# FNet mixing and a hard-swish MLP on one core: the first pair of batches handled one batch at a time

## The chip, the core and the metric

The kernel runs on one core of a Trainium2 chip. The core has TensorE (PE in the profile, its weight loads listed as PEld), VectorE (DVE), ScalarE (ACT), GpSimd (POOL) and SyncE (SP). Each engine works through its own instructions in program order and waits on semaphores for the others. DMAs are issued from the queues of SP, ACT and POOL and carried by 16 DMA engines. The metric is the device time of one execution in microseconds.

## The reference, cut to what matters

```python
# x: (8, 3008, 256) float32; w_in: (256, 2048) and w_out: (2048, 256), both float64
X = np.fft.fft(x, axis=1)
X = np.fft.fft(X, axis=2)
t = X.real.astype(np.float32).reshape(8 * 3008, 256)
h = t @ w_in
g = h * np.clip(h + 3.0, 0.0, 6.0) / 6.0
out = g @ w_out
```

## The kernel before, in words

The sequence of 3008 is split as 47 x 64. **Stage 1** is the Fourier sum over the 47 (its tables are `F`, and `F0` for the first pair), **stage 2** the one over the 64 with the twiddle factors (tables `T`). The transform over the 256 features is folded into `w_in`: the matrix `C` multiplies `w_in` on TensorE (`fold_w_in`, L663), and the result lies in `W1`. `w_in` and `w_out` come as float64. They are taken apart into exponent and mantissa by ScalarE, VectorE and TensorE (`exponent_a`, `exponent_b`, `exponent_c`, `mantissa`, `join`, L600 to L647) in 16 pieces, each brought in by `load_w` on POOL's queue. The real input's symmetry is used twice: a row and its partner are added and subtracted first (`fold`, L180), where the partner rows are gathered by an indirect DMA (`load_partners`, L170).

The eight batches form four pairs. For a pair, the rows of x are loaded in eight chunks of four columns of the 64 (`XC = 4`, `NXC = 8`), folded, put through stage 1, copied from PSUM to `z` by ScalarE, and written to memory as `zd` by SP. A group of four k1 is then read back as `g` (`load_g`, L305), transposed by the write and the read, and goes through stage 2 (`stage2`, L324), half a group for each call, into `q`. One row of q is needed on all partitions; `spread` (L354) writes it to memory and reads it back as a broadcast `qn`. For the first group `spread_by_pe` does that by products.

**The first pair** runs ahead of everything. Its two batches lie one under the other on 94 partitions, `stage1_first` (L253) multiplies by a block table of 94 x 96, and only the rows of group 0 are written at once. The rest stands in the list `later` and is written in the first MLP steps. Loads and gathers are all on POOL's queue, three chunks ahead. `keep_awake` (L687) issues products of zeros on TensorE: nine at the start, one after each of the first seven chunks.

**The MLP** runs over 4 pairs x 12 chunks (`ck`) x 8 steps (`fc`). A chunk is 4 k1-and-batch columns of 64 with their mirrored ones; before, two k1 for both batches. A step s issues, in the order written by hand:

- what `ahead` holds for it,
- `mlp1` of step s + 2: products u and v (L394) into one of three PSUM buffers, then `activate` on VectorE and ScalarE,
- what `behind` holds for it,
- `combine` of step s + 1 on POOL: three additions of 128 x 512 and 128 x 256 (L457),
- for the chunk before: `finish` at fc = 0 (five additions on POOL), `store` at fc = 1 and fc = 2 (two transposes on VectorE, L548, and eight output DMAs on SP, L554, each),
- `mlp2` of step s: seven products that add up over fc (L487).

The first eight steps (`first_steps`, `second_steps`) differ: the weights are finished between the products. `mix_w_out` makes four more blocks from `w_out` on POOL.

`beside` (L796) is the planner for all other work: `put(t, f, ...)` places a call in front of step t of the pair (or behind its mlp1 with `at=behind`). Stage 2 of later groups, their loads, and the next pair's x loads, folds (on POOL) and stage 1 (L223, four products of 47 rows in the four quarters of the array) are placed there. Since each engine keeps program order, an entry's DMAs stand on SP behind the outputs of earlier steps.

Pools matter as follows: `xpool` has four buffers for x, partners and some weight pieces; `ps_d` is one PSUM bank for stage 1, stage 2 and exponents; `ps_h` has three banks, for u and v first of all; `zpool`, `gpool` and `ypool` have two each.

Of the kernel before, what the change touches and what calls it, by code (L numbers as in the profile page):

```python
# [58 lines left out]
def kernel(  # L59
# [21 lines left out]
    PR0, PZ0 = 2 * N1, 2 * PZ  # L81
    XC = 4
    NS = N2 // 2
    NXC = NS // XC
    KC = 4
# [4 lines left out]
    NG = NCK // 2  # L90
    DH = 32
# [23 lines left out]
    F = consts.tile([P, 5 * PB], F32, name="F")  # L115
    F0 = apool.tile([PR0 + 2, 6 * PZ0], F32, tag="a", name="F0")
# [10 lines left out]
    class Pair:  # L127
        def __init__(self, p):
            self.p = p
            self.x, self.xr, self.y, self.z = {}, {}, {}, {}  # L130
            self.zd = self.zq = None
            self.g, self.q, self.qn = {}, {}, {}
# [3 lines left out]
    ORDER = [NXC - 1] + list(range(NXC - 1))  # L136

    def x_tile(pr, c):
        pool, tag = (spool, "t") if pr.p == 0 and ORDER.index(c) % 3 == 2 else (xpool, "x")
        return pool.tile([PX, XC, D], F32, tag=tag, name="xt")  # L140
# [8 lines left out]
    def load_forward(pr, c):  # L149
        xt = x_tile(pr, c)  # L150
        n = XC if c < NXC - 1 else XC - 1
        if pr.p == 0:
            o = xt[0:PR0 + 2]
            nc.gpsimd.dma_start(out=o[:, 0:n, :], in_=x_pn[0:PR0 + 2, c * XC + 1:c * XC + 1 + n, :])
            if n < XC:
                nc.gpsimd.dma_start(out=o[:, n:XC, :], in_=x_pn[0:PR0 + 2, 0:1, :])
        for b in range(2) if pr.p > 0 else ():
# [12 lines left out]
    def load_partners(pr, c):  # L170
        xr = x_tile(pr, c)
        pr.xr[c] = xr
        i = pr.p * NXC + c
        nr = PX if pr.p > 0 else PR0 + 2
        nc.gpsimd.indirect_dma_start(  # L175
            out=xr[0:nr].rearrange("p n d -> p (n d)"), out_offset=None, in_=x_r,
            in_offset=bass.IndirectOffsetOnAxis(ap=IX[0:nr, i:i + 1], axis=0),
        )

    def fold(pr, c, part, eng):  # L180
        nr = PX - 1 if pr.p > 0 else PR0
# [71 lines left out]
    def stage1_first(pr, c):  # L253
        y = pr.y.pop(c)
        n = XC if c < NXC - 1 else XC - 1

        def table0(i):
            return F0[0:PR0, i * PZ0:(i + 1) * PZ0]

        pt = ps_h.tile([P, 2 * TB], F32, tag="uv", name="pt")[0:PZ0]  # L260
        nc.tensor.matmul(pt[:, 0:n], table0(5), y[:, 0:n, P], start=True, stop=True)
        for k in range(2 if n < XC else 0):
            nc.tensor.matmul(pt[:, n:XC], table0(k + 1), y[:, n + k, P:P + 1], start=(k == 0), stop=(k == 1))

        k = ORDER.index(c)
        pool, tag = (zpool, "z") if k < 2 else (cpool, "c") if k < 5 else (qpool, "q") if k < 7 else (apool, "a")
        z = pool.tile([PZ0, XC, D + 1], F32, tag=tag, name="z")
        nc.scalar.copy(z[:, :, D], pt[:, 0:XC])
        for i in range(XC // 2):
            ps = bank([P, 2, D], "ps1")[0:PZ0]  # L270
            if (c, i) == (NXC - 1, XC // 2 - 1):
                nc.tensor.matmul(ps[:, 0], table0(0), y[:, 2 * i], start=True, stop=False, skip_group_check=True)
                for k, (j, cs) in enumerate([(XC - 1, slice(0, P + 1)), (XC, slice(0, P + 1)),
                                             (XC - 1, slice(P + 1, D)), (XC, slice(P + 1, D))]):
                    nc.tensor.matmul(ps[:, 1, cs], table0(k + 1), y[:, j, cs], start=False, stop=(k % 2 == 1),
                                     skip_group_check=True)
            else:
                nc.tensor.matmul(ps, table0(0), y[:, 2 * i:2 * i + 2, :], start=True, stop=True)
            nc.scalar.copy(z[:, 2 * i:2 * i + 2, 0:D], ps)
# [63 lines left out]
    def spread_by_pe(pr, gr, i, ps, copy=nc.scalar.copy):  # L343
# [7 lines left out]
        if i == 1:  # L351
            del pr.g[gr]
# [677 lines left out]
```

## Time and profile before

| what | value |
|---|---|
| three runs | 1940.03, 1940.06, 1939.75 us; median 1940.03 |
| span of the profiled execution | 1938.6 us |
| VectorE, stage 0 to 20 us / 20 to 40 / 40 to 56 / 56 to 80 | busy 13.0 / 15.2 / 13.7 / 22.6 us |
| DMA in the same stretches | 0.84, 230 GB/s / 0.85, 262 / 0.84, 274 / 0.55, 174 |
| POOL, 100 to 300 us | busy 167 of 200 us |
| L457, c<-a, POOL, 128 x 512 / 128 x 256 | 1250 / 716 ns each |
| L223, stage 1 product of a pair, PE | 601 ns each, 192 instructions |
| L187, L188, L193, L194, fold on POOL, 111 x 508 | 1229, 1058, 1263, 1264 ns |
| L187 and the like, fold on VectorE, 94 x 508 | 660 to 680 ns |
| L707, memset of 128 x 512, VectorE | 485 ns |
| L711, zeros into T, ScalarE | 2 x 2750 ns |
| L604, exponent, ScalarE | 764 ns each, two a piece |

"Busy" counts an engine's own instructions. A product of 32-bit numbers appears as two instructions of TensorE. In a timeline line the first number is the start, the second the extent in us, then engine, line, operation, what is written from what, and the count; in brackets stand idle time before it and what ended it.

### The profile page before, as it was taken

The page shows a single profiled execution, that of the slowest core. Times are in us where ns is not written, and L with a number is a line of the kernel's source. Part 1 is how long each engine was busy: PE and PEld are TensorE (multiplying, and loading weights), DVE is VectorE, ACT ScalarE, POOL GpSimd, SP SyncE. Part 2 cuts the span into 40 slices and gives each one's busy share as a digit, 9 for nine tenths or more (in the row PEclk, how much of TensorE's full clock was granted, in tenths as well). Part 3 has the DMA queues.
Part 4 walks back from the last instruction along what each step waited for, and adds up shares of the span by engine and source line. Part 5 has one row for each costly group of instructions (what it writes and reads, how often), then busy time and mean ns, then how long its engine had stood idle before and what let it go on. Part 6 is the DMA issues. An engine that isn't in the chain of part 4 may idle for free.

```text
span 1938.6 us, 27871 instructions
## 1 busy us (share of the span) xinstructions
PE 1922.3 (99%) x9220; PEld 1654.3 (85%) x9220; DVE 1438.2 (74%) x2780; ACT 679.9 (35%) x1161; POOL 1418.2 (73%) x1624
## 2 busy tenths in 40 slices
PE   9999999999999999999999999999999999999997
PEld 4688888888988888888898888888899888888887
DVE  7877777767777777777787777777778777777777
ACT  5634333333333333333333333333333333333332
POOL 4088888887678877787678877878666667666664
PEclk9999999999999999999999999999999999999999
DMA  8522221211112222121111221222110101101000
GB/s 248 177 60 63 59 53 50 55 46 33 35 34 58 67 56 55 44 52 33 34 36 49 53 55 44 52 53 50 35 28 20 28 17 28 34 11 28 21 18 20
DMA packets 149998, 96.57 MB, mean 50 GB/s; under 512 B 118991, under 2 KB 132307, under 8 KB 149854
## 3 DMA queue, kind: packets, MB, share of 16 engines
q1 hardware_dynamic: 138378, 57.57, 12.4%
q0 software_dynamic: 10816, 37.07, 6.7%
q8 instruction: 72, 1.18, 0.3%
q14 instruction: 72, 0.59, 0.1%
q10 hardware_dynamic: 660, 0.16, 0.0%
HBM read 57.44 MB, written 37.32 MB: 49 GB/s over the span
## 4 chain that ended last, share of the span: by engine, by line
PE 95%; DVE 2%; DMA 1%; issue 1%; ACT 1%; POOL 0%; SPq 0%; DVEq 0%; ACTq 0%; POOLq 0%
PE acc L487 56%; PE v L394 16%; PE u L394 16%; PE ps L337 2%; PE acc L467 1%; PE ps L223 1%; DVE a L443 1%; DMA xt<-in_x_dram,IX 1%; PE spare L673 1%; DVE s L403 0%; ACT t L440 0%; DVE o L548 0%; DVE u L424 0%; PE ex L621 0%; POOL xt L175 0%
## 5 line engine op out<-in xcount | busy, mean ns | idle before, releaser
L457 POOL TENSOR_TENSOR c<-a 128x512 f32<-128x512 f32 (+1 forms) x375 | 468.8, 1250 | 362.8 <-PE acc L487 312.4
L487 PE MATMUL acc<-c,G 128*128 128x256 f32 (+1 forms) x3008 | 696.9, 374 | 0.0
L440 ACT ACTIVATE t<-u,half 128x512 f32<-128x512 f32 (+1 forms) x384 | 260.6, 679 | 1141.9 <-DVE u L413 1058.9
L487 PEld LDWEIGHTS acc<-c,G 128*128 128x128 f32 x3008 | 565.4, 190 | 71.1
L403 DVE SCALAR_TENSOR_TENSOR s<-qn,WN,u 128x256 f32<-128x256 f32 (+1 forms) x768 | 330.6, 472 | 334.3 <-PE u L394 333.2
L487 PE MATMUL acc<-a,G 128*128 128x256 f32 (+1 forms) x2256 | 541.3, 375 | 0.0
L487 PEld LDWEIGHTS acc<-a,G 128*128 128x128 f32 x2256 | 421.5, 190 | 71.1 <-issue 17.5
L394 PE MATMUL v<-q,W 127*128 127x256 f32 (+1 forms) x1536 | 389.3, 375 | 3.0 <-DVE a L443 3.0
L394 PE MATMUL u<-q,W 128*128 128x256 f32 (+1 forms) x1536 | 388.0, 375 | 0.9 <-ACT q L340 0.9
L443 DVE SCALAR_TENSOR_TENSOR a<-t,u 128x512 f32<-128x512 f32 (+2 forms) x448 | 264.0, 601 | 102.3 <-ACT t L440 98.8
L394 PEld LDWEIGHTS v<-q,W 127*128 127x128 f32 x1536 | 287.8, 190 | 43.9 <-DVE a L443 3.6
L394 PEld LDWEIGHTS u<-q,W 128*128 128x128 f32 x1536 | 285.7, 190 | 37.6 <-issue 1.9
L457 POOL TENSOR_TENSOR c<-a,c 128x256 f32<-128x256 f32 (+1 forms) x375 | 268.6, 716 | 29.4
L457 POOL TENSOR_TENSOR c<-c,a 128x256 f32<-128x256 f32 (+1 forms) x375 | 268.5, 716 | 29.4
L413 DVE TENSOR_TENSOR u<-s,v 128x512 f32<-128x512 f32 x352 | 245.0, 696 | 36.7
L443 DVE SCALAR_TENSOR_TENSOR a<-t,v 128x512 f32<-128x512 f32 (+1 forms) x480 | 263.6, 566 | 0.3 <-ACT t L440 0.2
L440 ACT ACTIVATE t<-v,half 128x512 f32<-128x512 f32 (+1 forms) x384 | 260.5, 678 | 0.4 <-PE acc L487 0.2
L415 DVE TENSOR_TENSOR v<-v,s 128x512 f32<-128x512 f32 x352 | 243.9, 693 | 0.0
L457 POOL TENSOR_TENSOR r<-w,e 128x256 f32<-128x256 f32 (+1 forms) x92 | 88.7, 985 | 3.6
L497 ACT ACTIVATE e<-acc 128x512 f32<-128x512 f32 (+2 forms) x184 | 83.4, 544 | 0.0
L548 DVE STREAM_TRANSPOSE o<-r 128x256 f32<-128x256 f32 (+1 forms) x192 | 72.5, 415 | 0.2
L457 POOL TENSOR_TENSOR w<-w,e 128x512 f32<-128x512 f32 (+1 forms) x46 | 57.5, 1249 | 3.6
(110 smaller groups left out, 770.9 us busy)
## 6 DMA issues: line engine op xcount, KB each, us to landing
out_dram<-o SPq DMA_DIRECT2D x747, 32.0 KB
zd<-z SPq DMA_DIRECT2D x48, 192.0 KB
g<-zd SPq DMA_DIRECT2D x36, 256.0 KB
xt<-in_x_dram POOLq DMA_DIRECT2D x21, 256.0 KB
qn<-qd SPq DMA_DIRECT2D x19, 256.0 KB
st<-in_moe_w_in_dram POOLq DMA_DIRECT2D x8, 512.0 KB
st<-in_moe_w_out_dram POOLq DMA_DIRECT2D x8, 512.0 KB
xt<-in_x_dram POOLq DMA_DIRECT2D x17, 192.0 KB
```

The lines of the kernel that those rows point to most:

```text
L223: nc.tensor.matmul(ps[b][h * PB:(h + 1) * PB, 0:n], F[rows(b), 0:PB], y[rows(b), 2 * h:2 * h + n], start=True, stop=not last, skip_group_c ...
L337: nc.tensor.matmul(ps[:, blk, u * P:n].rearrange("p (b k) -> p b k", b=2), g[:, kk, blk * (P + 1):blk * (P + 1) + P], T[:, :, gr, blk, kk, ...
L394: nc.tensor.matmul(ps[:, i, 0:nq], W1[r, blk, f * P:(f + 1) * P], q[r, blk, of:of + nq], start=True, stop=True)
L403: nc.vector.scalar_tensor_tensor(s[:, i, 0:nq], qn[:, of:of + nq], WN[:, f:f + 1], u[:, i, 0:nq], op0=AL.mult, op1=AL.add)
L413: nc.vector.tensor_tensor(u[:], s[:], v[:], op=AL.add)
L415: nc.vector.tensor_tensor(v[:], v[:], s[:], op=AL.subtract)
L440: nc.scalar.activation(t, h, AF.Relu, bias=half[:], scale=scale)
L443: nc.vector.scalar_tensor_tensor(dst, t, 1.0, h, op0=AL.min, op1=AL.mult)
L457: (eng or nc.gpsimd).tensor_tensor(out, in0, in1, op=AL.add)
L487: nc.tensor.matmul(ch.acc[i // 2][:, i % 2, 0:ch.n], G[:, i, fc, :], mv, start=(fc == 0 and i % 2 == 0), stop=(fc == NF - 1), skip_group_c ...
L497: nc.scalar.mul(ch.e[:, k:i + 1, 0:ch.n], ch.acc[i // 2][:, 0:i + 1 - k, 0:ch.n], 1.0 / WS)
L548: nc.vector.transpose(o[:, 0:n // DH, h], ch.r[:, m, h, 0:n].rearrange("p (j i) -> p j i", i=DH))
```

## The change

The first pair is no longer handled as one. Its first batch alone goes through the early stage, its second batch is placed by `beside` between MLP steps. MLP chunks 0 to 3 of the first pair hold the first batch's sixteen k1 of groups 0 to 3, chunks 4 to 7 the second batch's, chunks 8 to 11 both batches as before.

- **Loads.** A load now holds columns of chunk m in partitions 0 to 46 and of chunk m + 4 in partitions 64 to 110: four loads, not eight. At the start the two halves go on SP's and ACT's queues, all four loads issued at once, and partners are gathered on POOL. For loads 1 to 3 partitions 32 to 63 are set to zero first. The second batch's halves both go on SP.
- **Fold.** For loads 1 to 3 of the first batch VectorE only adds the partner rows. The second addition and subtraction, of near and far columns, is done by TensorE, which adds up four products (table 6 is minus table 0).
- **Early stage 1** runs in the four quarters of the array; the last PSUM copy of the last load is on VectorE, and one of its two writes on ACT's queue.
- **Second batch.** Folds on POOL at steps 10 + 4k and 11 + 4k, stage 1 behind step 13 + 4k, with eight DMAs on SP each (nine for the one with the odd row).
- **Stage 2** by half groups, one batch each. The second chunk's, formerly done right after the first MLP products, is placed at step 4.
- **Others.** 13 warming products at the start and one after the first load; T's zeros are filled later; weight pieces 0 to 3 are issued behind the four gathers; exponents of pieces 2 and 3 on TensorE; `mix_w_out` at steps 4, 6, 8, 9; the next pair's loads at 24 + 6c instead of 8 + 8c; `F` has seven tables and is loaded once.

The diff, cut to its core:

```diff
+    def load_half(hb, m, queues, pool=xpool, tag="x", gap=False):
+        hb.x[m], hb.xr[m] = x_tile(pool, tag), x_tile(pool, tag)
+        if gap:
+            nc.vector.memset(hb.x[m][PB // 2:PB], 0.0)
+        for h in range(2):
+            c = m + h * NM
+            nr = N1 + 1 if h or gap else PB
+            n = XC if c < NXC - 1 else XC - 1
+            queue = queues[h]
+            rows, o = x_pn[hb.b * N1:hb.b * N1 + nr], hb.x[m][h * PB:h * PB + nr]
+            queue.dma_start(out=o[:, 0:n, :], in_=rows[:, c * XC + 1:c * XC + 1 + n, :])
+            if n < XC:
+                queue.dma_start(out=o[:, n:XC, :], in_=rows[:, 0:1, :])
+        gather(hb.xr[m], hb.b * NM + m)
+    def fold_half(hb, m, part, eng):
...
+        if hb.b == 0 and n == XC:
+            tt(a[:, :, 0:P + 1:P], a[:, :, 0:P + 1:P], r[:, :, 0:P + 1:P], op=AL.add)
+            return
...
+    def stage1_early(hb, m):
...
+        pt = [ps_h.tile([P, 2, 1], F32, tag="uv", name="pt") for h in range(2)]
+        ps = [bank([P, 2, D], "ps1") for h in range(2)]
...
+            for k, (t, to, fr) in enumerate([(0, cosine, cosine), (0, sine, slice(1, P)),
+                                             (0, slice(1, P), back), (6, sine, back)]):
+                for i, h, n in quarters:
+                    nc.tensor.matmul(ps[h][i * PB:(i + 1) * PB, :, to], table(t, h), y[rows(h), 2 * i:2 * i + 2, fr],
+                                     start=(k == 0), stop=(k > 1), skip_group_check=True)
...
+        nc.scalar.copy(z[:, 0, :, 0:D], ps[0][0:PX])
+        (nc.vector.tensor_copy if k == NM - 1 else nc.scalar.copy)(z[:, 1, :, 0:D], ps[1][0:PX])
...
+            (nc.scalar if k == NM - 1 and i else nc.sync).dma_start(out=dst[0:n0], in_=src[0:n0])
+            later.append((dst[n0:], src[n0:]))
+    def stage1_quarters(hb, m):
...
+            for h in range(2):
...
+                nc.sync.dma_start(out=zd[:].rearrange("g k c n d -> (g k c) n d")[:, n0:n0 + 2, 0:D], in_=z[r, h])
+                nc.sync.dma_start(out=zq[:, :, ::-1, n0:n0 + n].rearrange("g k c n -> (g k) c n"), in_=zc[r, h, 0:n])
+                if end:
+                    nc.sync.dma_start(out=zq[:, :, :, n0 + 1].rearrange("g k c -> (g k c)"), in_=z[r, h, 1, P])
+    def load_g_half(hb, gr):
+        g = gpool.tile([P, 2 * KK, D + 1], F32, tag="g", name="g")
+        zd = first.zd[hb.b][gr].rearrange("(u t) c n d -> (t c n) u d", t=2)
+        n = D if hb.b else D + 1
+        nc.sync.dma_start(out=g[:, 0:KK, 0:n], in_=zd)
+        if hb.b:
+            nc.sync.dma_start(out=g[:, 0:KK, D], in_=first.zq[gr].rearrange("(u t) c n -> (t c n) u", t=2))
+    def stage2_half(hb, gr, copy=nc.scalar.copy):
...
+        ps = bank([P, 2, TB], "ps2")
+        for u in range(KK):
+            for blk in range(2):
+                nc.tensor.matmul(ps[:, blk, u * P:(u + 1) * P].rearrange("p (b k) -> p b k", b=2),
+                                 g[:, u, blk * (P + 1):blk * (P + 1) + P], both_tables(gr, blk, u),
+                                 start=True, stop=True)
+        copy(first.q[vg][:, :, i * TB:(i + 1) * TB], ps)
+    def spread_half(hb, gr):
...
+        nc.sync.dma_start(out=qd[:, cs], in_=first.q[vg][P - 1:P, 1, cs])
+        nc.sync.dma_start(out=first.qn[vg][:, cs], in_=qd[:, cs].to_broadcast([P, TB]))
...
+            if pr.p == 0 and ck < 2 * NSG:
+                k1 = [ck % NSG * KC + j + 1 for j in range(KC)]
+                b = [ck // NSG] * KC
...
-    keep_awake(9)
+    keep_awake(13)
+    def load_first(k):
+        load_half(hb, ORDER[k], (nc.sync, nc.scalar), *((xpool, "x"), (xpool, "x"), (qpool, "q"), (apool, "a"))[k], gap=k > 0)
...
+    for k in range(NM):
+        load_first(k)
+        if k == 0:
+            nc.sync.dma_start(out=F[:], in_=c_stage1[:, 0:7 * PB])
...
+            put(1, load_g_half, halves[0], 1)
+            put(4, stage2_half, halves[0], 1)
+            put(5, spread_half, halves[0], 1)
+            for i, t in enumerate((4, 6, 8, 9)):
+                put(t, mix_w_out, i)
+            for gr in range(2, NSG):
+                put(8 * gr - 10, load_g_half, halves[0], gr)
+                put(8 * gr - 5, stage2_half, halves[0], gr)
+                put(8 * gr - 4, spread_half, halves[0], gr)
+            hb = halves[1]
+            for k, m in enumerate(ORDER):
+                t = 10 + 4 * k
+                put(t - 3, load_half, hb, m, (nc.sync, nc.sync))
+                for part in range(2):
+                    put(t + part, fold_half, hb, m, part, nc.gpsimd)
+                put(t + 3, stage1_quarters, hb, m, at=behind)
+            for gr in range(NSG):
+                put(8 * gr + 27, load_g_half, hb, gr)
+                put(8 * gr + 29 - (gr == 0), stage2_half, hb, gr)
+                put(8 * gr + 30 - (gr == 0), spread_half, hb, gr)
...
-                t = 2 * late + (9 - late // 4) * c
+                t = 9 * c if p > 0 else 24 + 6 * c
...
-    stage2(first, 0, 1, copy=nc.vector.tensor_copy)
-    spread_by_pe(first, 0, 1, spare[0][:, 0], copy=nc.vector.tensor_copy)
```

## The prediction

> **What bounds the kernel now.** I read the page first, then the chain of waits in order of time, then the timeline of the first 110 us and of two steps in the middle.
>
> ```profile
> span 1938.6 us, 27871 instructions
> PE 1922.3 (99%) x9220; PEld 1654.3 (85%) x9220; DVE 1438.2 (74%) x2780; ACT 679.9 (35%) x1161; POOL 1418.2 (73%) x1624
> ...
> PEclk9999999999999999999999999999999999999999
> ...
> PE 95%; DVE 2%; DMA 1%; issue 1%; ACT 1%; POOL 0%; SPq 0%; DVEq 0%; ACTq 0%; POOLq 0%
> ```
>
> TensorE carries 95% of the chain. So three things count: when its MLP work begins, how much is put between, and whether it ever waits. The chain shows the beginning:
>
> ```profile
> 29.73 0.68 DVE xt L187
> ...
> 32.93 1.81 PE ps L278 x4
> 34.74 0.02 issue
> 34.76 0.59 ACT z L279
> ...
> 43.54 0.28 ACT qn L350
> ```
>
> The eighth chunk of x arrives at 29.7, stage 1 ends at 34.7, its copy at 35.3; after that the chain is ScalarE's preparation of weights. The timeline has the first MLP product, and the start of TensorE:
>
> ```profile
> 1.68 9.57 PE L690 MATMUL awake<-Z,ones 128*128 128x512 f32 x18 [1.68 <-DVE half L701]
> 2.69 0.33 PEld L690 LDWEIGHTS awake<-Z,ones 128*128 128x128 f32 x1 [0.52 <-issue]
> ...
> 5.51 0.19 PEld L690 LDWEIGHTS awake<-Z,ones 128*128 128x128 f32 x1 [0.24 <-issue]
> ...
> 7.88 0.55 DVE L187 TENSOR_TENSOR xt<-xt 94x381 f32<-94x381 f32 x1 [3.53 <-DMA xt<-in_x_dram,IX]
> ...
> 43.60 1.13 PE L394 MATMUL u<-q,W 128*128 128x256 f32 x4 [0.95 <-ACT q L340]
> ```
>
> MLP products begin at 43.60. The warming products first come every 0.86 us a pass, then every 0.43.
>
> A step in the middle, with a stage 1 in it (step 17 of the second pair, fc = 1):
>
> ```profile
> 622.43 1.03 PE L394 MATMUL u<-q,W 128*128 128x256 f32 x4
> 627.54 0.79 SPq L240 DMA_DIRECT2D zd<-z  x2
> 628.40 1.03 PE L394 MATMUL u<-q,W 128*128 128x256 f32 x4
> 628.43 1.66 SPq L298 DMA_DIRECT2D zq<-zc  x2
> 630.19 11.31 SPq L554 DMA_DIRECT2D out_dram<-o  x16
> 633.15 1.05 PE L337 MATMUL ps<-T,g 128*128 128x128 f32 x8
> 633.16 0.76 DVE L548 STREAM_TRANSPOSE o<-r 128x256 f32<-128x256 f32 x2
> ```
>
> A plain step takes 4.75 us (628.40 to 633.15), one with a stage 1 takes 5.97, so a stage 1 costs 1.22. SyncE hands out DMAs one at a time: zd 0.40 each, zq 0.83, outputs 0.59 (median 0.537 by line, plus a gap); the sixteen outputs of a chunk take 9.5 us in most chunks, 11.3 here.
>
> **The change, part by part.**
>
> **1. The early x loads, folds and stage 1.** Eight chunks of 96 rows x 4 KB, twice (6.3 MB), become four of 112 rows, twice: 3.67 MB, with the 0.23 MB table. At the 230 to 262 GB/s of the first two 20 us stretches the last lands at 16.5 to 18.5, against 29.7. VectorE's fold shrinks from 2.75 us to two additions and a small one, 1.5 us. Three memsets of the gap rows (1024 columns at the 0.485 us of 512: 1.0 each) end near 7.4, hidden by the first load (7.88 before). Filling T's zeros (5.5 us on ScalarE) moves behind POOL's four gathers, to 8.5 to 14; hidden by the warming, as ScalarE has no z to copy before.
>
> TensorE now sets the pace. Thirteen warming products end at 11.25 + 4 x 0.86 = 14.7; the next can go in at 14.3. The first fold is ready by about 12 (7.9, some 0.4 for the larger chunk, 3.5 of operations). A later chunk is four products of some 258 columns in each quarter of the array instead of one of 512. L223 does four quarters of 512 columns in 0.85 plus a 0.24 tail, so two such amounts take 1.7, with the column and the tail 2.1. The first chunk has one amount, the odd row (L230, 1.04) and the column: 2.3. So 14.3 + 2.3 + 0.86 (one warming product) + 3 x 2.1 = 23.8. The trace has no products so short in quarters: by the one-column products of L263, one every 0.087 us, a chunk of 40 takes 3.5 and the stage ends at 28.9; with no limit by TensorE it ends 3.6 after the last load, at 20.1. I take 23.8, by L223, which uses the same quarters.
>
> From there to the first MLP product: copy 0.7; DMA issue on ScalarE 0.5; exponent 1.45 (before, it lay ahead of the last copies, at 32.09); its product 0.87; ex 0.58; then what followed in the old run from 35.82 to 43.60, 7.78, and 0.4 for the exponents of pieces 2 and 3, now products between the weight folds. 23.8 + 12.3 = 36.1. The load of g (zd 1.85, issue 0.65, landing 1.3) is ready near 28.3, and W pieces queued behind the gathers near 20 to 26: both lie under this. **Start: -7.5** (ends -11.2 and -2.4, by 20.1 and 28.9).
>
> The page titled "DMA: Bandwidth & Descriptors" of the Trainium skill (Issuing engines are not separate DMA queues) says that loads from several engines run on the same 16 DMA engines, and more queues save issue time only. The trace here has those engines 84% busy with the loads in one queue. I give the second queue nothing, and the sum stays.
>
> **2. The second chunk's stage 2 and row.** Their 1.06 + 0.61 of TensorE at 45.2 go; nothing is won, since v at 48.67 waits for VectorE anyway. VectorE loses two copies (1.1), worth 0 to 1.1 where TensorE waits on it at 64.0 to 66.4. A stage 2 comes back at step 4, 0.9 (158.77 to 163.53 against 164.41 with it), and up to 0.5 for the one PSUM bank. **+0.5** (-0.2 to +1.4).
>
> **3. Stage 1 of the second batch** goes into steps 13, 17, 21, 25: 3 x 1.22 + 1.67 for the one with the odd row (429.84 to 436.25 is 6.41 against 4.75). **+5.3.** Other stage 2 calls keep their number. Its folds go to POOL (5 us each, gather 1.0); rival three. Its eight loads go on SP, three steps ahead of their fold: 0.4 each to issue, behind at most 15 us of outputs, 14 us ahead; hidden, and if not, the fold is late, which POOL's slack takes. Copies on ScalarE (1.4 each) fit in its 65% idle. Spreads are twice as many on SP, 0.6 each.
>
> **4. The wait at step 28.** Step 25 has the last stage 1 of batch two. It issues four zd and four zq DMAs on SP, not two and two. Behind them stand step 25's eight outputs and step 26's eight; then, at step 27, the load of g that stage 2 needs as the first work of step 28. From the start of step 25: first zd at 5.1 (622.43 to 627.54); 4 x (0.40 + 0.83) and gaps, 10.3; sixteen outputs 9.5, 19.8; two loads 0.62 + 0.61, 21.1; landing 1.3 (POOL's last g issue ended at 39.75, the read began at 41.05), 22.4. TensorE is at step 28 after 5.97 + 2 x 4.75 = 15.5. **+6.9.** Lower end: the second eight outputs cannot go before step 26's transposes (633.92, that is 11.5), so 11.5 + 4.75 + 1.3 + 1.3 = 18.8, a wait of 3.3. Upper, with 11.3 for the outputs: 8.7. It cannot be a gain; TensorE is in order and everything behind it waits. The later loads (35, 43, 51) are used two steps after, not one: the outputs end 15.2 after the step with fc = 1 begins, 18.0 with the load, and stage 2 comes at 19.0 or later (at 53, with a stage 1 among the outputs, 20.7 against 21.1). So they only just come in time.
>
> **5. TensorE's clock after that wait.** The first four passes of warming took 0.43 us too long each, 1.7 together. The longest idle time without such a loss is 2.4 us (64.0 to 66.4). A wait of 6.9 lies between; **+0.85**, the middle of 0 and 1.7.
>
> The skill's page "TensorE: Matmul & The Clock Gate" (Part 1: The HAM clock gate) says an idle window of about 3.4 us halves the clock until a busy one has passed. By it the loss is the whole 1.7 and the time 1946.9; no run here shows such an idle time.
>
> Sum: -7.5 + 5.3 + 0.5 + 6.9 + 0.85 = +6.05; 1938.6 + 6.05 = 1944.65. The median of the runs lies 1.4 above the profiled span: **1946.1**.
>
> **Rivals.**
>
> *One, not slower: no wait at step 28.* If SP hands the load out in time, -7.5 + 5.3 + 0.5 = -1.7: 1938.3, and 1934.6 with the fast start (-11.2). For it: TensorE waits for no g in the old steady state. Against: those loads had seven steps. It decides once SP needs under 10 us rather than 17 from the first zd to the landing.
>
> *Two, early stage 1 bound by issue:* start -2.4, so +11.15, 1951.2. For: forty small products a chunk, a row of 0.087. Against: L230's sixteen take 1.04.
>
> *Three, POOL bounds steps 10 to 25.* Its additions take 2.68 us a step, 4.65 a chunk for finishing; 16 steps need 52, and 24 for four folds and gathers, of 82. Six us spare; where they bunch with a finish, as at 16 and 24, up to 6 stand ahead of the additions; the old step 16 had 2.1 + 4.65 there and TensorE did not wait. From step 24 the next pair's folds come every six steps, not eight: 26.7 of 29.7. If an addition beside them runs a quarter longer, some 4 are lost: 1950.
>
> *Four, two queues don't do what they say:* the gathers, still on POOL, get a third of the DMA engines beside two hardware queues and FI comes late; first fold ready at 15.5, not under 14.3: +1.2, 1947.3.
>
> **How the numbers follow.** What a measurement of this kernel can tell from no change is about 0.2%, 3.9 us: 1936.1 to 1943.9. The forecast has 0.50 (0.42 slower, 0.08 within when the start is fast and the wait short), its own range 1941 to 1950. Rival one 0.26 (0.13 within, 0.13 faster); two 0.10, slower; three 0.08 (0.07 slower); four 0.06 (0.04 slower). Faster 0.13, within 0.24, slower 0.63. Range: 1935.5 to 1952, from rival one's fast half to rival two.
>
> **What would show it.** Step one: first u near 36.1; TensorE's last early stage 1 near 23.8. Step three: steps of 6.0 at 13, 17, 21, 25. Step four: an idle time of TensorE near 7 us at about 204 us (step 8 began at 109.07; 7 less, then 17 steps, two stage 2 and three stage 1 more, then three steps), ended by g's DMA, with SP busy with outputs before it; five: passes of 0.43 becoming 0.86 behind it. Without that idle time the forecast is wrong, and rival one holds; a first u after 40 speaks for rival two, TensorE waiting for c at L487 for three.

## The result, and the profile after

The changed kernel takes 1957.4 us (median of 4 runs, 1953.9 to 1959.0) against 1940.05: 0.85% slower, ratio 1.0085 (95% interval 1.0071 to 1.0100). The profiled execution is the slowest of the four, with a span of 1957.3 us against 1938.6. "Slower" was right, 1946.1 was 11 us too little, and the range ended at 1952.

The page of the changed kernel, the lines that answer to those shown before:

```profile
span 1957.3 us, 28195 instructions
PE 1925.8 (98%) x9344; PEld 1658.0 (85%) x9344; DVE 1425.2 (73%) x2757; ACT 680.2 (35%) x1165; POOL 1430.2 (73%) x1638
...
PEclk8999999999999999999999999999999999999999
...
PE 94%; DVE 3%; DMA 1%; ACT 1%; issue 0%; SPq 0%; POOL 0%; DVEq 0%; ACTq 0%; POOLq 0%
```

TensorE still carries the chain, but the first slice of its clock has fallen from 9 to 8. To find where the time went I set the start of each of the 384 products u of the changed kernel against the same product of the kernel before; where the difference jumps, time was lost or won. (There is one u a step, and after the first chunk it is issued two steps ahead of its own.)

| place | difference of start | jump | predicted |
|---|---|---|---|
| first u (38.26 against 43.60) | -5.3 | -5.3 | -7.5 |
| third u (57.95 against 59.97) | -2.0 | +3.3 | 0 |
| second chunk's stage 2, all jumps | | +1.7 | +0.5 |
| stage 1 of the second batch, steps 13 to 25 | | +5.3 | +5.3 |
| step 12, TensorE waits for POOL's c | | +1.9 | 0 (rival three) |
| step 28, wait for g and the clock behind it | | +9.1 | +6.9 + 0.85 |
| steps 37 and 45, waits for g | | +0.55, +1.8 | 0 |
| two small jumps, 0.12 and 0.26 | | +0.4 | 0 |
| sum, flat behind step 75 | +18.7 | | +6.05 |

The start, in the timeline of TensorE (start, duration, engine, line, operation, in brackets the idle time before it and what ended it):

```profile
26.51 1.23 PE L742 MATMUL ex<-PM,E 128*128 128x512 f16 x2 [3.14 <-ACT PM L730]
27.53 3.62 PE L811 MATMUL awake<-Z,ones 128*128 128x512 f32 x4
...
38.26 1.13 PE L520 MATMUL u<-q,W 128*128 128x256 f32 x4 [0.39 <-ACT q L434]
...
44.96 1.53 PE L520 MATMUL v<-q,W 127*128 127x256 f32 x4 [3.84 <-DVE a L569]
```

The last early stage 1 ends at 23.4, near the forecast's 23.8. Then TensorE idles 3.14 us, and four warming products take 3.62 us, nearly twice the 1.88 that they take at the full clock. A second gap of 3.84 stands before the third u. The windows (stretch, its length, busy time of PE, PEld, DVE, ACT, POOL with counts, granted clock, DMA share, GB/s) show the clock at 0.51 and 0.69 behind the two gaps; between them it was 1.00:

```profile
28.00:32.00 4.00, 4.00 (x7) 1.51 (x6) 0.69 (x1) 1.68 (x3) 0.00 (x0) 0.51 0.52 158
...
44.00:48.00 4.00, 3.04 (x7) 1.79 (x8) 3.36 (x7) 3.42 (x6) 0.72 (x1) 0.69 0.02 5
```

What ended the second gap stands in the chain of waits:

```profile
36.75 5.35 DMA WN<-W
...
42.12 0.49 DVE s L529
```

WN is one row of the folded weights, turned into columns; VectorE needs it for `s`. WN<-W is a transfer of 0.5 KB, and it took 5.35 us. POOL issued four transfers of 512 KB (weight pieces 6 to 9) from 35.61 to 38.49, the first two ahead of it:

```profile
35.61 1.44 POOL L714 DMA_DIRECT2D st<-in_moe_w_out_dram  x2
37.05 1.44 POOL L710 DMA_DIRECT2D st<-in_moe_w_in_dram  x2
```

The DMA engines were 74% busy from 36 to 40 and 82% from 40 to 44.

Step 28, from the timeline of TensorE and of SyncE's issues:

```profile
198.33 1.09 PE L357 MATMUL ps<-y,F 47*64 47x512 f32 x8
201.13 0.32 SPq L377 DMA_DIRECT2D zd<-z  x1
...
206.88 9.37 SPq L680 DMA_DIRECT2D out_dram<-o  x16
216.35 0.41 SPq L412 DMA_DIRECT2D g<-zd  x1
...
219.01 2.07 PE L431 MATMUL ps<-T,g 128*128 128x128 f32 x8 [6.87 <-DMA g<-zd]
220.88 1.91 PE L520 MATMUL u<-q,W 128*128 128x256 f32 x4
...
226.71 1.03 PE L520 MATMUL u<-q,W 128*128 128x256 f32 x4
```

This is step four of the prediction to the letter: eight small writes, sixteen outputs in 9.4 us, then the load, and TensorE idle for 6.87 us (7.27 counted for its weight loads). Stage 2 then takes 2.07 us where 1.05 is its time. The window behind the wait shows the clock at 0.50:

```profile
219.00:223.00 4.00, 3.98 (x13) 3.55 (x14) 0.17 (x1) 0.58 (x1) 0.00 (x0) 0.50 0.00 0
```

Step 45 repeats it in small (load issued at 304.85, a wait of 1.54 and no loss of clock), and POOL has a line of its own at step 12:

```profile
132.34 2.31 PE L613 MATMUL acc<-c,G 128*128 128x256 f32 x8 [1.34 <-POOL c L583]
```

### The profile page after: what moved, and what is told of

Same layout as the page of the kernel before. It is cut to its first block, busy times and chain, and to the rows that moved or that the text cites. A ratio compares the mean times of both kernels' runs of the same rounds, so it can differ in the third digit from the quotient of the medians.

```text
span 1957.3 us, 28195 instructions
## 1 busy us (share of the span) xinstructions
PE 1925.8 (98%) x9344; PEld 1658.0 (85%) x9344; DVE 1425.2 (73%) x2757; ACT 680.2 (35%) x1165; POOL 1430.2 (73%) x1638
## 3 DMA queue, kind: packets, MB, share of 16 engines
q1 hardware_dynamic: 143378, 60.56, 12.7%
HBM read 58.27 MB, written 37.32 MB: 49 GB/s over the span
## 4 chain that ended last, share of the span: by engine, by line
PE 94%; DVE 3%; DMA 1%; ACT 1%; issue 0%; SPq 0%; POOL 0%; DVEq 0%; ACTq 0%; POOLq 0%
PE acc L613 55%; PE v L520 16%; PE u L520 16%; PE ps L470 2%; PE ps L271 1%; PE acc L593 1%; PE awake L811 1%; DVE a L569 1%; DVE s L529 1%; ACT t L566 1%; DMA WN<-W 0%; DMA g<-zd 0%; DMA zd<-z 0%; DVE o L674 0%; DVE u L550 0%
```

## The experiments

Each run starts from the changed kernel. Besides the time, the table gives the starts of the first and third u, as the start varies from run to run. Where no number of runs stands, there was one (the kernel before has the median of four); the kernel before, run beside these, took 1940.8 to 1941.3 us (medians).

| run | first u | third u | third minus first | us |
|---|---|---|---|---|
| before | 43.60 | 59.97 | 16.37 | 1940.05 |
| changed | 38.26 | 57.95 | 19.69 | 1957.4 (4 runs) |
| e_stage2_29 | 37.72 | 58.75 | 21.03 | 1952.1 |
| e_g_act | 37.37 | 53.14 | 15.77 | 1942.6 |
| e_awake_wait | 37.88 | 57.07 | 19.19 | 1955.2 |
| e_awake_start | 38.06 | 53.83 | 15.77 | 1954.3 |
| e_wn_first | 38.29 | 54.06 | 15.77 | 1953.3 |
| e_weights_later | 36.85 | 56.22 | 19.37 | 1956.1 |
| e_stage2_6 | 38.65 | 58.27 | 19.62 | 1959.2 |
| e_mix_early | 36.96 | 55.58 | 18.62 | 1954.1 |
| e_one_queue | 37.21 | 52.98 | 15.77 | 1954.1 |
| h_four | 36.84 | 52.61 | 15.77 | 1941.4 (11 runs) |
| h_five | 38.13 | 53.90 | 15.77 | 1942.6 (11 runs) |
| h_early_exponent | 38.80 | 54.57 | 15.77 | 1941.25 (11 runs) |
| h_c_by_pool | 37.04 | 52.81 | 15.77 | 1939.7 (11 runs) |
| h_weights_last | 35.51 | 51.28 | 15.77 | 1938.0 (11 runs) |

**The wait at step 28.** Three runs: ask for g later, load it from another queue, fill the wait.

```diff
-                put(8 * gr + 29 - (gr == 0), stage2_half, hb, gr)
-                put(8 * gr + 30 - (gr == 0), spread_half, hb, gr)
+                put(8 * gr + 29, stage2_half, hb, gr)
+                put(8 * gr + 30, spread_half, hb, gr)
```

> The second batch's first stage 2 and its spread go one step later (steps 29 and 30 in place of 28 and 29), as those of its other groups stand. Theory (a late load: g lands at 216.8 to 219 whatever TensorE does, and TensorE comes to it too early): TensorE has the 5.5 us of step 28 to do first, so the 6.9 us wait shrinks to 1 to 2 us and the clock stays at 1.00; from the second batch's first group on, the products start 6 to 8 us less late, and the time is about 1950. Rival (what is lost there is DMA contention and the stage's own work, not the place of the wait): the wait goes along to step 29 at nearly its length, the time within 2 us of 1957. Either way nothing changes before 212 us.

```profile
219.69 1.16 PE L431 MATMUL ps<-T,g 128*128 128x128 f32 x8 [2.39 <-DMA g<-zd]
```

g came when it came before; the wait is 2.39, a little over the 1 to 2 us expected, the clock stays at 1.00 in every window from 200 to 227, and the products stand 6.4 us less late from step 29 on (1.1 more at step 45). The theory holds. The time is 1952.1 and not 1950, as the third u came 0.8 later than in the changed kernel.

```diff
-        nc.sync.dma_start(out=g[:, 0:KK, 0:n], in_=zd)
+        queue = nc.scalar if hb.b else nc.sync
+        queue.dma_start(out=g[:, 0:KK, 0:n], in_=zd)
...
-            nc.sync.dma_start(out=g[:, 0:KK, D], ...)
+            queue.dma_start(out=g[:, 0:KK, D], ...)
```

> The loads of g of the second batch are issued by ScalarE, all else is as in the changed kernel. Theory (queue order: the load stands behind 16 outputs that SP issues in 9.4 us): the writes of zd and zq are issued by 206.8 and land about 2 us later, so g lands by about 212; the waits of 6.9, 0.55 and 1.8 us at steps 28, 37 and 45 go, and with the first of them the clock loss of 1.85; time 1945 to 1949. Rival (the DMA engines are full with the outputs, so g lands late from any queue): less than 3 us of it comes back. A danger to both: ScalarE itself stands at the load until the writes have landed, some 2 us, and if TensorE's products of the next step wait for it, up to 2 us are given back.

```profile
201.71 9.42 SPq L681 DMA_DIRECT2D out_dram<-o  x16
202.48 0.40 ACTq L413 DMA_DIRECT2D g<-zd  x1
...
206.82 1.05 PE L432 MATMUL ps<-T,g 128*128 128x128 f32 x8
```

With the outputs under way in SP's queue, ScalarE's load goes out at once and TensorE does not wait at all. Against the changed kernel 9.1 us come back at step 28, 0.55 at 37, 1.78 at 45: 11.4 in all. The outputs did not hold the DMA engines, only SP's place in line; the rival falls. The danger named did not show: ScalarE's next activation, at 204.84, waited for VectorE and not for the load. (This run also had the better start of the table, worth 5.2 us until there, though its code is the same at that place; the rest of its gain is this.)

```diff
+                if gr == 0:
+                    put(28, keep_awake, 6, W1[:, 0, 0:2 * TB])
                 put(8 * gr + 29 - (gr == 0), stage2_half, hb, gr)
```

> Twelve products that nothing reads (six calls, about 5.1 us at the full clock) stand ahead of the second batch's first stage 2, inside its wait; the load of g stays as late as it was. Theory (the clock falls because TensorE idles for 6.9 us, and that costs 1.85 us after the wait): g still lands at about 219, the wait that is left is 1.5 to 2.5 us, the clock stays at 1.00 from 219 to 223, stage 2 takes 1.05 in place of 2.07 us and the next product 1.03 in place of 1.91; the products from there on start about 1.9 us earlier, time 1.9 less than the changed kernel. Rival (stage 2 is slow for another reason, its operands or the DMAs beside it): the stage keeps its 2.07 us and the time is unchanged within 0.3.

```profile
211.27 5.31 PE L811 MATMUL awake<-W,ones 128*128 128x512 f32 x12
218.59 1.16 PE L431 MATMUL ps<-T,g 128*128 128x128 f32 x8 [2.00 <-DMA g<-zd]
...
224.34 1.03 PE L520 MATMUL u<-q,W 128*128 128x256 f32 x4
```

The load is as late as ever, but stage 2 now takes 1.16 and the clock is 1.00 from 219 to 223 (0.50 in the changed kernel). The products come back by 0.59 and 1.07 there, 1.66 in all. Measured against TensorE's own products the load was 0.3 us later in this run; from the start of stage 2 to the second u behind it the changed kernel takes 7.70 us and this run 5.75. So **the clock by itself costs 1.7 to 1.95 us**, and the wait the other 7.1 to 7.4.

**The start.**

```diff
+    keep_awake(3)
     load_g_half(hb, 0)
```

> Three more calls of keep_awake (six products, 2.6 us) follow the last early stage 1, where TensorE of the changed kernel was idle from 23.4 to 26.5 us and the clock was 0.50 until 32. Theory (the idle gap costs half the early gain): clock 1.00 until 32, the two later calls take 1.7 in place of 3.4 us, the first product u comes 1 to 2 us earlier than 38.26, then it is bound by g, which landed at 35.1; the second u, held by WN, 1 to 2 us earlier as well; time 1 to 2 less. Rival (the late DMAs of g and WN set the start, the clock is covered by them): first u within 0.4 us of 38.26 and time unchanged within 0.5.

```profile
24.49 2.84 PE L811 MATMUL awake<-Z,ones 128*128 128x512 f32 x6
27.85 1.88 PE L811 MATMUL awake<-Z,ones 128*128 128x512 f32 x4
36.22 1.16 PE L431 MATMUL ps<-T,g 128*128 128x128 f32 x8 [1.31 <-DMA g<-zd]
```

The clock holds, yet the first u gains 0.2 only: g, landing at 36.2, is what it waits for now. The third u gains 4.1. For the third u the theory is right, by more than it said: with the clock held the second fold of W ends early enough for WN to go out before the weights, which wait for g. The first u lies in the rival's range, but one run doesn't decide it, as the last early stage 1 ended 1.2 us later here (24.6 against 23.4). Counted from that end, the first u comes 13.1 to 14.9 us later in the six runs whose first gap cost the clock, and 13.0 to 13.5 in the three that held it with the transfers in the same order (this one, e_g_act and h_four): what the clock is worth there isn't settled beyond that.

```diff
-    see(hb.g[0][:, 0, 0:1])
-    for j in range(6, 8):
-        load_w(j)
...
     fold_w_in(1)
+    see(WN[:, NF:NF + 1])
+    for j in range(6, 8):
+        load_w(j)
```

> Weight pieces 6 and 7 are loaded only once the second column of WN has landed, in place of once g has. Theory (the second WN transfer took 5.35 us because it was issued behind these 1 MB of weights, and the idle TensorE then lost the clock a second time): it lands in about 2 us, the third product u comes 3 to 4 us earlier (near 54) even if the clock falls at 24 to 32 as it did in the changed kernel, no half clock from 44 to 50; what may come back is at most 2 us, where ScalarE meets pieces 6 and 7 before they have landed. Rival (WN is late for other reasons, the queue of SP or the writes of z): it lands at about 42 again and the third u stays at 57 to 59.

```profile
27.72 3.26 PE L811 MATMUL awake<-Z,ones 128*128 128x512 f32 x4
...
42.76 1.13 PE L520 MATMUL v<-q,W 127*128 127x256 f32 x4 [1.61 <-DVE a L569]
```

Here the clock fell at the first gap as in the changed kernel and the first u came no earlier, but the third came 3.9 earlier. That is the theory's 54, and it settles the second loss: it is the 0.5 KB transfer behind the weights. (Pieces 8 and 9, no longer held by the wait for g, went out at 27.6 and 30.1 here.) In the table every version of the change has either 15.77 us between first and third u, or 18.6 to 21.0; nothing lies between.

```diff
         if k == 1:
-            for j in range(4, 6):
-                load_w(j)
+    keep_awake(3)
...
-    for j in range(6, 8):
+    for j in range(4, 8):
         load_w(j)
```

> As the run with three more calls of keep_awake at the start, and weight pieces 4 and 5 (1 MB) are loaded with 6 and 7 in place of inside the early stage 1. Theory (g lands at 35 because the writes of z share the DMA engines with the weights): z's writes land 2 to 2.5 us earlier, g by about 33, TensorE's wait of 1.3 us for it in the run with keep_awake alone goes, and the first u comes at 36.6 to 37.2 in place of 38.06; the four pieces then stand before or beside WN, so that the third u may come later than 53.8. Rival (what makes g late is SP's own chain of writes and the round trip, not the weights): g lands within 0.7 us of 35.5 and the first u within 0.5 of 38.06.

First u at 36.85, no wait for g, as the theory had it; the four pieces then met WN, and the third u came 19.37 behind, though the clock had held up to the first u. g took 2.8 us from its issue at 31.27.

```diff
-        load_half(hb, ORDER[k], (nc.sync, nc.scalar), ...)
+        load_half(hb, ORDER[k], (nc.sync, nc.sync), ...)
...
+    keep_awake(3)
```

> As the run with three more calls of keep_awake at the start, and the early loads of x all go through SP's queue, in place of row halves in SP's and ScalarE's. Theory (a second queue adds nothing, as the same DMA engines carry both): the first fold, the last early stage 1 and the first u come within 0.6 us of those of that run. Rival (one queue hands the rows out too slowly, or ScalarE's own queue brings its half earlier): first fold 1 to 3 us later, and the last early stage 1 later by as much, up to what TensorE's warming products cover (they end at about 14.5).

VectorE's first addition of the first and of the last of the four chunks, with one queue:

```profile
8.87 0.56 DVE L207 TENSOR_TENSOR xt<-xt 111x381 f32<-111x381 f32 x1 [1.09 <-DMA xt<-in_x_dram,IX]
...
21.08 0.69 DVE L207 TENSOR_TENSOR xt<-xt 111x508 f32<-111x508 f32 x1 [2.19 <-DMA xt<-in_x_dram]
```

With two queues these stand at 11.06 and 19.66 in the changed kernel, 11.74 and 20.90 in e_awake_start. One queue serves the first chunk 2 to 3 us sooner and the last somewhat later; the warming products cover the first, so the last early stage 1 ends within 0.2 us (the next products begin at 24.66 against 24.49) and the first u is 0.85 earlier, inside what that start varies by (38.06 in e_awake_start, 36.84 in h_four with the same start). So the theory's 0.6 us holds for the last early stage 1 alone, and the first fold, which the rival had later with one queue, came sooner. The second queue reorders the loads, and no gain of it shows.

**Step 4 and step 12.**

```diff
-            put(4, stage2_half, halves[0], 1)
-            put(5, spread_half, halves[0], 1)
+            put(6, stage2_half, halves[0], 1)
+            put(6, spread_half, halves[0], 1)
```

> Stage 2 and spread of the second chunk go from steps 4 and 5 to step 6, where no exponent product needs the one PSUM bank that stage 2 leaves its sums in. Theory (the wait of 0.87 us of the exponent product for ScalarE's copy of q is the bank's): the sixth product u comes 1.7 to 1.8 us earlier against the fifth than in the changed kernel, of which stage 2's own 0.9 us comes back by the ninth, so that 0.8 to 0.9 us stay; time 0.9 less, the start apart. Rival (the wait is ScalarE's load, not the bank, and moves along, or the later spread makes the ninth product's follow-up late): no more than 0.3 us stay, or the ninth u comes later by up to 3.

The sixth u gains 1.77 against the fifth, the eighth gives back 0.90: 0.87 stays. That is what the bank cost in the changed kernel's profile, where the exponent's product waits 0.72 us for ScalarE's copy of q. It isn't a fixed price: in six of the eight other runs made from the changed kernel with stage 2 still at step 4 (e_g_act and e_stage2_29 among them) the sixth u lost 0.57 us less, which leaves 0.3 for the bank. The time is no less: this run lost 0.67 at the 27th u, waiting for VectorE, as e_awake_wait (0.75) and e_mix_early (0.58) did too. Why either differs between runs is open.

```diff
-            for i, t in enumerate((4, 6, 8, 9)):
+            for i, t in enumerate((4, 5, 6, 7)):
```

> POOL mixes the output weights at steps 4, 5, 6 and 7 in place of 4, 6, 8 and 9. Theory (TensorE's 1.9 us at step 12 is POOL's backlog: without a pause from 105.6 to 129.5 us, two mixes of 3.1 us among it, ahead of the odd chunk's fold): the wait of 1.34 us for c goes, and the sixteenth u comes 1.7 to 2.0 us earlier against the fifteenth; time 1.9 less, the start apart. Rival (what is late is the gather's issue and its wait, 0.28 and 0.97 us, or DVE before it): at least 1 us of the 1.9 stays. A danger to both: in steps 5 and 7 POOL's mixes slow VectorE or hold up a load of weights, and products before the ninth come later.

The first chunk's later products read blocks that are already mixed here, so this run tells times only. The sixteenth u comes 1.92 earlier against the fifteenth, and no product before it later. So the 1.9 us is POOL's backlog, and the mixing is what piles it up.

**Parts together.** h_four joins e_g_act, e_awake_start and e_stage2_6 with the odd chunk moved back by one step:

```diff
-                t = 10 + 4 * k
+                t = 10 + 4 * k + (k == 0)
```

> Four edits together: g of the second batch loaded by ScalarE, three more calls of keep_awake behind the early stage 1, stage 2 and spread of the second chunk at step 6, and the odd chunk of the second batch folded, loaded and transformed one step later (its fold at steps 11 and 12, stage 1 at 14), which takes POOL's backlog away without touching the mixing. Theory (the parts add): against the changed kernel's profile -11.1 at the three waits for g, -4.1 to -4.7 at the start, -0.9 at step 6, -1.9 at step 12; span about 1939, time 1939 to 1941.5, the ratio to the kernel before 0.999 to 1.001, and runs that lie within 2 us of one another where the changed kernel's spread over 5. Rival (what is won at one place is lost at the next, because TensorE's earlier calls meet transfers that are not ready): 1943 or more. POOL's part alone may fail, as the fold then stands nearer to stage 1: then a wait for y at step 14 of 1 to 2 us.

1941.4 us, ratio to before 1.0006 (0.9994 to 1.0018); ten of eleven runs between 1941.0 and 1942.0, one at 1952.9, which has no profile. Step 6 and the three waits came as expected, and the start gained 5.3 us by the third u where 4.1 to 4.7 were expected; of POOL's 1.9 us only 0.5 came back (0.3 was lost before and 1.1 a step later, with a wait of 0.55 for c).

> As the run with four edits, and weight pieces 4 to 7 are loaded only once the second column of WN has landed. Theory: g lands at about 33.5 and WN in 2 us, as each of the two did where it was freed alone, so the first u comes at 36.8 to 37.2 and the third at 52 to 52.7 (38.06 and 53.83 with keep_awake alone); time 1 to 1.7 us less than with four edits, 1937.5 to 1940, that is 0.9985 to 1.000 of the kernel before. Rival (the pieces now come too late for ScalarE's exponents of pieces 4 and 5): a wait of 1 to 3 us for them behind the first u, and no gain or a loss against four edits.

A miss: 1942.6 us, ratio 1.0005 (0.9996 to 1.0014). WN was free (15.77), but g took 3.8 us from its issue, with a wait of 1.47 and the first u at 38.13, although e_weights_later had moved the same pieces and had g early. The rival's wait for late pieces did not show either: the third u came 15.77 us behind the first, and the ninth still stood 1.2 us behind h_four's.

h_early_exponent takes the last mixing to step 12 in place of the fold's move, lets pieces 6 and 7 wait for WN as e_wn_first does, and reorders the start:

```diff
         if k == 0:
-            nc.sync.dma_start(out=C[:], in_=dim)
-            load_t(0)
+        if k == 2:
+            exponent_a(0)
...
+    nc.sync.dma_start(out=C[:], in_=dim)
+    load_t(0)
     load_g_half(hb, 0)
...
-    head(0)
+    head_b(0)
     exponent_b(0)
-    keep_awake(1)
+    keep_awake(3)
     exponent_c(0)
     head(1)
     join(0)
-    keep_awake(1)
     exponent_b(1)
```

> As the run with four edits, with other means at three places: the odd chunk's fold stays where it was and the last mixing goes from step 9 to 12 instead; ScalarE computes the first exponent before the copies of the last early stage 1, and three calls of keep_awake stand behind its product; C and T are loaded behind the last write of z, which waited 4 us for C to land, and weight pieces 6 and 7 behind WN. Theory (the chain from the last early stage 1 to the first u is ScalarE's and g's, and both have room): ScalarE's chain 1.5 to 2 us earlier, g issued at 28 to 30 in place of 32.3, first u at 34.5 to 36 in place of 36.84; the wait for c at step 12 gone, 1.0 less than there; span 1936 to 1938, time 1937.5 to 1939.5, ratio 0.998 to 0.9995. Rival (something else, such as the weights' transfers, sets g's landing and now C's as well): first u at 36.5 or later, time 1940 to 1942.

```profile
31.10 3.39 PE L795 MATMUL wps<-wi,C 128*128 128x256 f32 x8 [2.34 <-DMA C<-in_c_dim_dram]
```

The exponent's product moved up by 1.9 us, and g's load went out at 30.44 in place of 32.3, but C, now issued at 26.3, became the late transfer: a wait of 2.34, and the fold of W at half clock (3.39 for 1.89). First u 38.80 and 1941.25 us, ratio 1.0000 (0.9991 to 1.0009): the rival's figures. The wait for c at step 12 is gone.

Two causes of a late g were open now: SP's last write of z, which had waited 3 to 4 us for C in the changed kernel, e_weights_later, h_four and h_five, and the weights. In h_c_by_pool C goes through POOL, ahead of the weights:

```diff
+    nc.gpsimd.dma_start(out=C[:], in_=dim)
     for j in range(4):
         load_w(j)
...
-    nc.sync.dma_start(out=C[:], in_=dim)
     load_t(0)
```

> As the run with the early exponent, and C is loaded by POOL ahead of the weights (at about 9 us) in place of by SP behind the last write of z. Theory (SP's last write of z waited for C, which the weights held up to 28.7; and in the run with the early exponent C, issued at 26.3, landed at 31 and took TensorE 2.3 us and the clock): C is there by 18, no wait of the first fold of W, no half clock; the last write of z goes out at 26, g at about 30.4, landed by 33.5; first u at 34.5 to 35.7 in place of 38.80; span 1936 to 1937, time 1937.5 to 1939, ratio 0.9975 to 0.999. Rival (the weights' transfers set the start in any order: 256 KB more ahead of x make x and the early stage 1 later by 1 us, g lands at 35 as in the other runs): first u at 36.5 to 38, time 1939.5 to 1942.

```profile
27.04 0.72 POOL L711 DMA_DIRECT2D st<-in_moe_w_in_dram  x1 [8.10 <-DVE top L754]
28.79 0.72 POOL L711 DMA_DIRECT2D st<-in_moe_w_in_dram  x1 [1.03 <-ACT PM L731]
...
30.07 0.40 SPq L413 DMA_DIRECT2D g<-zd  x1
...
35.24 1.13 PE L432 MATMUL ps<-T,g 128*128 128x128 f32 x8 [1.78 <-DMA g<-zd]
```

1939.7 us, ratio 0.9993 (0.9984 to 1.0002). SP's writes of z end at 26.4 in place of 29.3: that wait was real and is gone. But g, issued 2.2 us earlier than in the changed kernel, let stage 2 start 5.2 us later only, and the first u at 37.04 lies in the rival's range, as the time does. The lines show what stands ahead of g: pieces 8 and 9, at 27.04 and 28.79. So they did in h_five (27.8 and 30.2), while they came behind g in e_weights_later. The last run moves these two behind WN as well:

```diff
-    head_b(0)
+    mantissa(0)
...
-    head(1)
+    exponent_a(1)
+    mantissa(1)
...
-    for j in range(6, 8):
+    for j in range(6, 10):
         load_w(j)
```

> As the run with C by POOL, and weight pieces 8 and 9 too are loaded only once the second column of WN has landed. With WN as POOL's gate instead of g they had gone out at 27.0 and 28.8, just ahead of g. Theory (g's load took 5.1 us there, 3.8 with five edits and 2.6 to 2.9 in every run in which pieces 8 and 9 stood behind g, so they are what held it up): g is issued at about 30 and landed by 33, TensorE waits for it 0.3 us or less, the first u comes at 34.7 to 35.4, the third 15.77 us behind it; span 1936 to 1937, time 1937.5 to 1939, ratio 0.998 to 0.9995. Rival (g needs until 35 for another reason): first u at 36.8 or later, time as the run before, 1939.7 or more, as the later weights may be missed. A danger to both: pieces 8 and 9 late for the exponents of step 2.

```profile
30.86 0.40 SPq L413 DMA_DIRECT2D g<-zd  x1
...
33.70 1.13 PE L432 MATMUL ps<-T,g 128*128 128x128 f32 x8 [0.85 <-DMA g<-zd]
...
35.51 1.13 PE L521 MATMUL u<-q,W 128*128 128x256 f32 x4 [0.23 <-ACT q L435]
```

g takes 2.8 us, the first u comes at 35.51 and the third at 51.28, both 1.53 earlier than with C by POOL. The weights it was. The time is 1938.0 us (one of the eleven runs took 1945.7) against 1941.2 for the kernel before, run beside it, ratio **0.9987 (0.9978 to 0.9996)**: the one version whose whole interval lies ahead of the kernel before, by about 2.5 us, which is less than the 0.2% that the prediction took for telling a change from none.

## Why the prediction was wrong

**The start, step one, failed, and it is the largest miss.** Its first half held: last early stage 1 at 23.4 for 23.8, the second queue worth nothing. (The rule of the Trainium skill, "DMA: Bandwidth & Descriptors", Issuing engines are not separate DMA queues, holds by e_one_queue's 24.66 against 24.49; rival four's sign, a late first chunk, was there too, 11.06 against 8.87, and hidden.) The second half, "23.8 + 12.3", summed ScalarE's work and left out what TensorE does meanwhile. Three things are missing in it.

First, TensorE idles 3.1 us there, and the clock it loses makes the warming products 1.7 longer. The sum's own terms, 0.7 + 0.5 + 1.45 from the copy to the exponent, say that TensorE has nothing to do for 2.65 us; I priced a lost clock at step 28 and did not look for a gap in my own new start. Second, "the load of g is ready near 28.3 ... both lie under this" is wrong by 7 us: g came at 35.1 in the changed kernel, and in seven of the eight runs in which the clock held from there to the first u, TensorE waited 0.2 to 1.8 us for it. In the changed kernel SP stood 3.9 us at a write of z until C had landed, then 2.7 until the writes had, and the load took 2.8 from its issue where the sum had 0.65 + 1.3; weights issued just ahead of g held it longer in h_five and h_c_by_pool. Third, nothing in the sum asked what the earlier start would meet: WN behind the weights, +3.3 at the third u, by e_wn_first a matter of the order of issue.

The gain of 7.5 was within reach, and more (the first u at 35.51 in h_weights_last, 8.1 ahead of the kernel before, the ninth 8.7), but the change as made kept 1.2 of it by the ninth u. How much it keeps varies: with the same code up to there, the third u was 6.8 ahead of the kernel before in e_g_act and 1.2 in e_stage2_29. Six runs share that code: in e_g_act the clock held and the third u came 15.77 us behind the first, in the other five the clock fell and it came 18.6 to 21.0 behind. That is the likeliest reason why the changed kernel's own runs spread over 5 us; I have no profile of each of them.

**Step two, +0.5,** had its mechanism right and its size low for this run: the bank cost 0.87, not "up to 0.5". In six other runs it cost 0.3, inside the forecast.

**Step three, +5.3,** was right for stage 1 (the jumps are 1.22 and 1.66). Its POOL half was wrong: rival three, at 8%, happened in part. I counted folds, gathers and additions over 16 steps and found 6 us to spare, but left out that the mixing at steps 8 and 9 (3.1 us each) comes just before, so that POOL enters step 10 without a pause since 105.6. It cost 1.9 us, and moving the mixing gave 1.92 back in e_mix_early.

**Step four, +6.9,** was right: 6.87, the place, the queue and the cause, confirmed from three sides (asked later, another queue, filled). Of the 18.7 us, 9.1 are lost at step 28, enough by itself for "slower"; the losses that the sum did not have would have made the profiled run slower too. What it called "only just in time" was late by 0.55 and 1.8: those loads should have been terms of the sum and not a remark. It had the numbers: a load ready at 18.0 against a use at 19.0, counted from the step with fc = 1. At step 37 the loads were issued by 16.0, but the last landed 3.7 us later and not 1.3, at 19.7; at step 45 the sixteen outputs took 11.5 us and not 9.5 besides. The load with the narrower margin, 20.7 against 21.1, made no wait.

**Step five, +0.85,** was mis-sized: the middle of 0 and 1.7, and the upper end was true, or a little low: 1.66 us came back in e_awake_wait, 1.95 is the difference from stage 2's start. The Trainium skill ("TensorE: Matmul & The Clock Gate", Part 1: The HAM clock gate) says that an idle window of about 3.4 us halves the clock. This trace agrees: after 6.87 us without a product the granted clock was 0.50. By that rule the prediction had the whole 1.7 as a loss, near the 1.66 to 1.95 measured.

**Rivals one and two** did not happen: there was a wait, and forty small products a chunk took 1.95 us, not 3.5.

So of the 12.7 us by which the profiled span exceeds the forecast's (18.7 for 6.05), about 5.5 are the start's, 2.3 the later loads of g, 1.9 POOL, 1.4 step 28 and its clock, 1.2 the second chunk's stage 2, 0.4 small jumps without a cause found.

## What to carry to other kernels

When a stage is moved earlier, list what its successor will now meet: which transfers are still running, which are issued just before the small one it needs, and how long TensorE will idle in the new order. A load that waited in a queue behind outputs was cured here by another engine's queue, for nothing, as that engine could afford to stand at the load until the data was there; filling the gap with unread products bought back only the clock. And "just in time" in a sum is a term with two ends, not a remark.

## What was not expected of the hardware

Gaps of about 2.4 us can cost the clock. Idle times of 2.40, 2.46, 2.76, 2.90, 3.06 and 3.14 us of TensorE before the first exponent's product were each followed by warming products of 2.8 to 3.6 us in place of 1.88; one of 2.39 was not (1.88, in e_g_act, with the same code there), nor did the waits of 2.39 in e_stage2_29 and 2.00 in e_awake_wait cost it. A wait of 2.34 in h_early_exponent did (3.39 for 1.89). The Trainium skill ("TensorE: Matmul & The Clock Gate", Part 1: The HAM clock gate) says that activity is judged in free-running windows of about 3.4 us. That gaps of 2.39 and 2.40 us had opposite outcomes agrees with the free running; that 2.3 us can be enough does not agree with a wholly idle window.

A 0.5 KB transfer issued among four of 512 KB took 5.35 us, and g's load of 257 KB took 5.2 us right behind two of 512 KB, 2.6 to 3.0 without them. A queue of its own was no protection: the weights came from POOL, g and WN from SP.
